# Chunk 12 transposed on TensorE, loads moved behind transposes, and a rearranged start, in a retention and hard-swish kernel

## The chip, the cores and the metric

The kernel runs on one core of a Trainium2 chip. The core has TensorE (matrix products, which write PSUM), VectorE (DVE in the profile), ScalarE (ACT), GpSimd (POOL) and SyncE (SP), each with its own instruction stream in program order, and 16 DMA engines that move data between memory (HBM) and the on-chip SBUF. DMAs are issued from the queues of SP, ACT and POOL. The engines meet by semaphores. The metric is device microseconds of one execution; less is better.

## The reference

```python
def _attn_ref(q, k, v):                       # each 8 x 8 x 576 x 64: batch, heads, positions, head size
    scores = scale * np.matmul(q, k.transpose(0, 1, 3, 2))
    gamma = 1.0 - 2.0 ** (-5.0 - np.arange(H, dtype=np.float32))
    rel = pos[:, None] - pos[None, :]
    Dmat = np.where(rel >= 0, gamma[:, None, None] ** rel[None, :, :], 0.0)
    return np.matmul(scores * Dmat, v)

def _moe_ref(x, w_in, w_out):                 # x 4608 x 512, w_in 512 x 2048, w_out 2048 x 512
    h = x @ w_in
    g = h * np.clip(h + 3.0, 0.0, 6.0) / 6.0
    return g @ w_out
```

A decayed causal attention without softmax (retention) for 8 batch entries and 8 heads, its heads laid side by side to rows of 512, and then two dense layers with a hard swish between them.

## The kernel before, in words

**Tiling.** Tokens are worked on in nine blocks of 512. Block 0 holds the first 64 positions ("heads" in the code) of all eight batch entries; blocks 1 to 8 hold the other 512 positions of one batch entry each, as four chunks of 128. Chunks are numbered through: 4 to 35, and chunk c belongs to block c // 4. For each chunk the retention is computed inside the chunk with a mask, and what lies before it comes in through a state of 64 x 64 per head that is decayed and carried on.

**One chunk.** `load(c)` (L171) puts three loads into SP's queue: keys, queries and values as fp32 (tiles fk, fq, fv; `IOB` = 4 buffers each, 256 KB a load). `casts(c)` (L182 to L184) makes fp16 of them: keys on ACT, queries and values with their decays on POOL. `transposes(c, on_pe)` turns k and q so that the head size lies on partitions. With `on_pe` it is done by TensorE against an identity (tiles ptk and ptq, L161), and copied out of PSUM by ACT (k) and VectorE (q) (L195). Without it, SP issues two DMA transposes (L197). `state(c)` (L243 to L249) forms the next state: products on TensorE, a sum on VectorE, a decay on POOL. `past(c)` (L235) has ACT put a state into the tile sbd. `scores(c)` (L208, L211) forms the products of qT and kT and masks them on VectorE. `inner(c)` (L262, L161, L266) forms the chunk's output, which ACT copies into xT, the input of the dense layers.

**The dense layers.** `up_steps` does one of 16 units of 128 hidden columns for a block: four products of w_in and xT into a PSUM bank (ph), u by ACT (L387), g by VectorE (L389). `down_plain` does the second layer for blocks 0 and 1, one product at a time (a "D" of the plans, pd), the other blocks use a Strassen scheme (`down_strassen`, pm) with sums of weights that VectorE makes (L405, "+n" in the plans). Weights come by POOL's queue, converted to fp16 by the DMA: w_in in four pieces (`win_piece`, L508) and w_out in four (`wout_piece`, L511). The queue stands in program order behind the heads' keys and values (L293).

**Order.** The order of everything is written out by hand. For blocks 0 to 2 strings say it: "k0 D4 ... t11 c13" means: item k for 0, four D, ..., the transposes of chunk 11 on TensorE, cast of chunk 13. The letters: c cast, t transposes on TensorE, s state, z past, a scores, i inner, k and h the heads' keys and states, o a kept output store of block 0, U, L and R whole and half units of the up layer. An engine executes its share of the items in this order. From block 2 on, tables give the order.

**Queue order on SP.** `cast(c)` also feeds SP: for c >= `PE_T` it issues the DMA transposes of c, and then `fetch(c + IOB + 1)` loads up to chunk c + 4:

```python
PE_T = 12
...
            if c >= PE_T:
                transposes(c, False)
            fetch(c + IOB + 1)
```

So chunks 4 to 11 are turned by TensorE, chunks 12 to 35 by DMA. The first four chunk loads are held until the third w_out piece has landed (`fetch(8, wout[2])`).

**The start.** Keys and queries of block 0 come in quarters (one pair of heads): head pair 0's keys and all queries by SP and ACT as fp32, cast on the chip (`cast_heads`, L304); keys of pairs 1 to 3 and all values by POOL's queue with conversion to fp16 in the DMA. `turn_heads` transposes a pair on TensorE (L311) and copies it out (L315); `scores_heads` masks with hmask, which ACT makes by exponentials (`mask_of_heads`, L122). `idle_products` are products without use that keep TensorE busy. `others()` (L125 to L141) makes the decay tables on VectorE and ACT, multiplies the heads' keys by decays on POOL, and clears or fills small tiles.

Of the kernel before, what the change touches and what calls it, by code (L numbers as in the profile page):

```python
# [15 lines left out]
ACTF = mybir.ActivationFunctionType  # L16
ALU = mybir.AluOpType
# [4 lines left out]
def kernel(  # L22
# [9 lines left out]
    nc = tc.nc  # L32
    B, H, S, D = q.shape
    NTOK, DM = out.shape
    DFF = moe_w_in.shape[1]
    P = 128
    NP = H // 2
    NFC = DFF // P
    BLK = 512
# [16 lines left out]
    IOB = 4  # L56
# [64 lines left out]
        for h in (2 * i, 2 * i + 1):  # L121
            nc.scalar.activation(hmask[:, h, :], dist, ACTF.Exp, bias=scale, scale=float(np.log(gamma[h])))  # L122

    def others():
        for h in range(H):  # L125
            lg = float(np.log(gamma[h]))
            nc.vector.tensor_scalar(arg[:, :, h], fj[:, 0:NJ + 1], lg, float(np.log(D ** -0.5)),
                                    ALU.mult, ALU.add)
            nc.vector.tensor_scalar(arg[:, :, H + h], fj[:, 0:NJ + 1], -lg, 0.0, ALU.mult, ALU.add)
        nc.scalar.activation(dec, arg, ACTF.Exp)  # L130
        for i in range(NP):
            k16 = hd[i]["k"].rearrange("p e j d -> p j e d")
            dd = dec[:, 0:NJ, H + 2 * i:H + 2 * i + 2].unsqueeze(3).to_broadcast([P, NJ, 2, D])
            nc.gpsimd.tensor_tensor(k16, k16, dd, ALU.mult)
        for i in range(2):
            nc.vector.memset(sbd[i], 0.0)
        nc.vector.tensor_copy(only[:, 1:2], odd)
        nc.vector.tensor_scalar(only[:, 0:1], odd, -1.0, 1.0, ALU.mult, ALU.add)
        for h in range(H):
            lo = (h % 2) * D  # L140
            nc.vector.memset(gpow[lo:lo + D, h // 2:h // 2 + 1], float(gamma[h] ** P))  # L141

    def mask_of_chunk():
        nc.gpsimd.memset(mask, 1.0)
# [125 lines left out]
    def idle_products(n):  # L270
        idle = psum.tile([P, NP, P], FP32, tag="pp", name="idle")
        for _ in range(n):
            product(idle, ident16, ident16.unsqueeze(1).to_broadcast([P, NP, P]), start=True, stop=True)
# [11 lines left out]
    def load_half(i, nm, e, queue, behind=None):  # L285

        if nm not in hd.setdefault(i, {}):
            if queue is nc.gpsimd:
                hd[i][nm] = heads16(i, nm)
            else:  # L290
                f = io.tile([P, H, D], FP32, tag=f"f{nm}", name=f"h{nm}{i}")
                hd[i][nm] = f.rearrange("p (e j) d -> p e j d", e=2)
        d = queue.dma_start(hd[i][nm][:, e].rearrange("p j d -> p (j d)"),  # L293
                            dict(q=q, k=k, v=v)[nm][:, 2 * i + e, 0:TL, :].rearrange("b (r j) d -> r b (j d)", j=NJ))
        if behind is not None:
            after(d, behind)
        return d
# [4 lines left out]
    def cast_heads(i, nm, copy):  # L302
        t = heads16(i, nm)
        copy(t, hd[i][nm])  # L304
        hd[i][nm] = t

    def turn_heads(i, nm, copy):
        pt = psum.tile([P, NJ, P], FP32, tag="st", bufs=2, name=f"hpt{nm}{i}")
        for j in range(NJ):
            for e in range(2):  # L310
                nc.tensor.matmul(pt[e * D:e * D + D, j, :], hd[i][nm][:, e, j, :], by_chunk, start=True, stop=True,  # L311
                                 skip_group_check=True)
        x, y = (NCB, 2 * RP) if nm == "k" else (2 * NCB, RP)
        t = work.tile([P, x, NJ, y], FP16, tag=f"{nm}T", bufs=4, name=f"h{nm}T_{i}")
        copy(t, pt.rearrange("p j (x y) -> p x j y", y=y))  # L315
        hd[i][nm + "T"] = t
# [186 lines left out]
                pend.append((ws[n][:, j, :], x[:, j, :], y[:, j, :], op))  # L503


    def win_piece(n):
        a, b = pieces_in[n]
        return nc.gpsimd.dma_start(win16[n], win_v[:, :, BLK * a:BLK * b])  # L508

    def wout_piece(pc):  # L510
        return nc.gpsimd.dma_start(wout16[:, JQ * pc:JQ * pc + JQ, :], wout_v[pc])  # L511

    PE_T = 12
    loaded, ready = [NCB], [NCB]

    def fetch(n, behind=None):
        while loaded[0] < min(n, NCH):
            for i in load(loaded[0]):
                if behind is not None:
                    after(i, behind)  # L520
            loaded[0] += 1

    def cast(c):
        if c < NCH:
            assert ready[0] == c
            casts(c)
            ready[0] += 1
            if c >= PE_T:
                transposes(c, False)
            fetch(c + IOB + 1)  # L530

    def do(todo):
        for what, c in todo:
# [36 lines left out]
    with tc.manual_schedule(engines={ENG.PE, ENG.DVE, ENG.Pool, ENG.Activation, ENG.SP}):  # L570
        sp, act, pool = nc.sync, nc.scalar, nc.gpsimd
        on_act, on_dve = nc.scalar.copy, nc.vector.tensor_copy
        indices()
        for nm in ("k", "q"):
            load_half(0, nm, 0, sp)
            load_half(0, nm, 1, act)
        nc.scalar.activation(warm, half, ACTF.Exp)
        load_half(1, "q", 0, sp)
        load_half(1, "q", 1, act)
        for i in (2, 3):  # L580
            for e in range(2):
                load_half(i, "q", e, sp)
        for i, nm in ((1, "k"), (2, "k"), (3, "k"), (0, "v"), (1, "v"), (2, "v"), (3, "v")):
            for e in range(2):
                load_half(i, nm, e, pool)
        win_piece(0)
        distances()
        idle_products(5)
        mask_of_heads(0)
        cast_heads(0, "k", on_dve)  # L590
        turn_heads(0, "k", on_act)
        for i in (1, 2, 3):
            mask_of_heads(i)
        idle_products(2)
        cast_heads(0, "q", on_dve)
        turn_heads(1, "k", on_act)
        cast_heads(1, "q", on_dve)
        turn_heads(0, "q", on_dve)
        turn_heads(1, "q", on_act)
        cast_heads(2, "q", on_dve)  # L600
        turn_heads(2, "k", on_act)
        scores_heads(0)
        cast_heads(3, "q", on_act)
        scores_heads(1)
        turn_heads(3, "k", on_act)
        turn_heads(2, "q", on_act)
        values_heads(0)
        turn_heads(3, "q", on_act)
        scores_heads(2)
        values_heads(1)  # L610
        inner_heads(0, on_act)
        scores_heads(3)
        values_heads(2)
        inner_heads(1, on_act)
        win_piece(1)
        values_heads(3)
        inner_heads(2, on_dve)
        first = [up_steps(0, u) for u in range(3)]
        for dmc in range(3):
            for unit in first:  # L620
                next(unit)
            if dmc == 1:
                inner_heads(3, on_act)
        for unit in first:
            for _ in unit:
                pass
        for n in (2, 3):
            win_piece(n)
        wout = [wout_piece(pc) for pc in (0, 2, 1, 3)]
        mask_of_chunk()  # L630
        others()
        fetch(8, wout[2])
        for u in range(3, NFC):
            up_unit(0, u)
        weight_sums(4, 7)
        weight_sums(6, 3, 1)
        down = down_plain(0)
        go("k0 D4 k1 D4 +1 k2 D4 +1 k3 D6 h0 D2 c4 +1 h1 D3 z4 h2 D3 +1 h3 D3 c5 D4 t4 D5 s4 a4 D5 t5 +1 i4 "
           "z5 c6 D4 s5 a5 D7 i5 D2 t6 z6 L2 c7 s6 a6 L3 D3 t7 L1 i6 L3 a7 z7 L3 c8 D2 i7 D3 t8 R3 c9 R3 "
           "s8 a8 z8 R2 t9 R2 c10 i8 R2 U1 s9 a9 z9 c11 U3 i9",  # L640
           1, down)
        down = down_plain(1)
        go("t10 c12 z10 D6 s10 a10 D2 t11 c13 +1 D6 i10 z11 D1 a11 c14 +2 D8 i11 z12 o1 +1 D6 D1 s12 a12 c15 D4 +1 "
           "D4 i12 z13 o1 D1 s13 a13",
           down=down)
        go("U1 D3 i13 U1 D2 U1 z14 U1 D2 s14 a14 U1 D2 c16 U1 D2 i14 U1 D2 z15 U1 D2 +1 U1 a15 D2 "
           "U1 D2 c17 +1 U1 D2 i15 +1 U1 D2 +1 U1 +1 U1 D2 U1 U1",
           2, down)
        for kb in range(2, NB):
            for _ in down:  # L650
                pass
            plain = kb < FIRST
            down = down_plain(kb) if plain else down_strassen(kb)
            per = 4 if plain else 7
            table = FIRST_STEADY if kb == 2 else STEADY
            c = NCB * (kb + 2)
            for u in range(NFC):
                lead = per - 2 if u == 0 else 0
                for _ in range(lead):
                    next(down, None)  # L660
                if kb + 1 < NB:
                    up_unit(kb + 1, u)
                else:
                    side_sums(1)
                for _ in range(per - lead):
                    next(down, None)
                do((w, i if w == "+" else c + i) for w, i in table.get(u, []))
        for _ in down:
            pass
# [30 lines left out]
```

## Time and profile before

| | |
|---|---|
| time, three runs | 306.31, 306.67, 307.20 us (median 306.67) |
| profiled execution | 307.96 us, of which the span is 306.3 us |
| TensorE busy | 289.8 us (95%) |
| VectorE, ACT, POOL busy | 240.1, 200.0, 146.5 us |
| longest wait of TensorE | 4.6 us, scores on a DMA transpose of q |
| other waits of TensorE over 1 us | 1.9 (start), 1.8 (heads' keys), 1.4 (w_in) |
| SP's transposes | 24 of k, 24 of q; median 4.3 and 3.0 us from issue to landing |
| chunk loads on SP | 96, 256 KB each, median 4.3 to 5.3 us to landing |

Times in the profile are us from the start of the span. In the lists of waits a line says: engine, tile and line, "<-" what it waited for, then us in total, how often, and the longest. In the table of windows each row has the window, its length, and for PE, PEld (weight loads), DVE, ACT and POOL the busy time and the count of instructions; the last three numbers are the granted TensorE clock as a share of full speed, the busy share of the DMA engines and GB/s. In a timeline a row has start, us, engine, line, operation, output <- inputs, shapes and how many were merged; in brackets the idle time before it and what ended it. "SPq" is an issue on SP's queue, which takes SP the time given; the landing comes later.

### The profile page before, as it was taken

The numbers are of one execution on the slowest core, as the hardware profiler recorded it, in microseconds if no ns is written. First come the engines' busy times: TensorE is split into PE (matmuls) and PEld (weight loads), VectorE is DVE, ScalarE is ACT, GpSimd is POOL, SyncE is SP. The second block draws the span as 40 slices with busy tenths as digits, with TensorE's granted clock in tenths as the row PEclk, the third lists the DMA queues.
The fourth block names the chain that finished last, engine by engine and source line by source line (L and its number), as shares of the span: only waits on it lengthen the run. The fifth ranks groups of instructions, "written<-read, shape, count | busy, mean of one in ns | idle before, by whom it ended". The sixth has DMA issues, their size and how long they took to land.

```text
span 306.3 us, 10639 instructions
## 1 busy us (share of the span) xinstructions
PE 289.8 (95%) x4494; PEld 223.9 (73%) x4494; DVE 240.1 (78%) x414; ACT 200.0 (65%) x373; POOL 146.5 (48%) x153
## 2 busy tenths in 40 slices
PE   4889999999949999999999999999999999999994
PEld 1668566887625667778787878787887878778893
DVE  4749486888934795989979987989798979777962
ACT  5748867999725686875677577657766765455330
POOL 7815097636740900984197519743973353013100
PEclk9799999999998999999999999999999999999999
DMA  6999999999999999999979997897925000300123
GB/s 150 191 206 215 197 205 214 215 213 209 172 146 235 204 218 225 161 175 225 217 167 160 198 210 151 147 205 195 153 54 173 20 19 2 140 2 2 68 74 137
DMA packets 137072, 48.01 MB, mean 157 GB/s; under 512 B 126784, under 2 KB 131904, under 8 KB 137024
## 3 DMA queue, kind: packets, MB, share of 16 engines
q1 hardware_dynamic: 131888, 41.83, 69.7%
q0 software_dynamic: 4704, 5.11, 10.1%
q8 instruction: 35, 0.57, 0.8%
q10 hardware_dynamic: 432, 0.39, 0.5%
q14 instruction: 13, 0.11, 0.1%
HBM read 36.70 MB, written 9.44 MB: 151 GB/s over the span
## 4 chain that ended last, share of the span: by engine, by line
PE 83%; DVE 5%; DMA 5%; POOL 2%; ACT 2%; issue 1%; POOLq 0%; DVEq 0%; ACTq 0%
PE ph L161 39%; PE pm L161 28%; PE pd L161 7%; PE pa L208 3%; PE po L262 2%; PE po L161 2%; DMA win<-in_moe_w_in_dram 2%; DMA hk<-in_k_dram 2%; DVE g L389 2%; DMA qT<-q 1%; DVE ws L405 1%; ACT u L387 1%; DVE a L211 1%; POOL hk L293 1%; PE pu L243 1%
## 5 line engine op out<-in xcount | busy, mean ns | idle before, releaser
L161 PE MATMUL ph<-xT,win 128*64 128x512 f16 (+1 forms) x1248 | 148.1, 367 | 2.2 <-DMA win<-in_moe_w_in_dram 1.4
L387 ACT ACTIVATE u<-ph,half 128x512 f32<-128x512 f32 (+1 forms) x156 | 100.0, 656 | 65.1 <-PE ph L161 63.1
L389 DVE SCALAR_TENSOR_TENSOR g<-u,ph 128x512 f16<-128x512 f32 (+1 forms) x156 | 98.1, 642 | 38.6 <-ACT u L387 38.0
L161 PEld LDWEIGHTS <-win 128*64 128x64 f16 x1248 | 82.6, 137 | 26.7 <-issue 2.3
L249 POOL TENSOR_TENSOR z<-t,gpow 128x256 f32<-128x256 f32 x24 | 18.0, 750 | 81.3 <-DVE t L248 73.1
L161 PEld LDWEIGHTS <-g 128*64 128x64 f16 x704 | 38.3, 110 | 14.8 <-issue 0.7
L211 DVE TENSOR_TENSOR a<-pa,mask 128x512 f16<-128x512 f32 x64 | 40.3, 682 | 5.1 <-PE pa L208 5.1
L161 PE MATMUL pm<-ws,s 128*64 128x256 f16 x672 | 43.8, 273 | 0.0
L161 PEld LDWEIGHTS <-s 128*64 128x64 f16 x672 | 37.0, 110 | 7.1
L405 DVE TENSOR_TENSOR s<-g 128x1024 f16<-128x1024 f16 x42 | 41.3, 987 | 0.0
L184 POOL TENSOR_TENSOR v<-fv,dec 128x512 f16<-128x512 f32 x32 | 40.0, 1250 | 0.1
L183 POOL TENSOR_TENSOR q<-fq,dec 128x512 f16<-128x512 f32 x32 | 37.4, 1167 | 1.9 <-DMA fq<-in_q_dram 1.9
L161 PE MATMUL pd<-wout,g 128*64 128x512 f16 x256 | 34.6, 386 | 0.0
L161 PE MATMUL pm<-ws,g 128*64 128x256 f16 x448 | 30.6, 273 | 0.0
L161 PE MATMUL pm<-wout,sab 128*64 128x256 f16 x448 | 30.6, 273 | 0.0
L161 PEld LDWEIGHTS <-sab 128*64 128x64 f16 x448 | 24.7, 110 | 4.8
L266 ACT CAST xT<-po 128x512 f16<-128x512 f32 x32 | 18.8, 587 | 13.1 <-PE po L161 13.0
L405 DVE TENSOR_TENSOR sab<-g 128x1024 f16<-128x1024 f16 x28 | 23.4, 838 | 0.0
L182 ACT CAST k<-fk 128x512 f16<-128x512 f32 x32 | 19.8, 619 | 0.2
L235 ACT CAST sbd<-z 64x256 f16<-64x256 f32 x48 | 19.2, 400 | 0.4
L262 PE MATMUL po<-a,v 128*64 128x128 f16 x256 | 18.5, 219 | 0.3 <-DVE a L211 0.3
L161 PE MATMUL po<-qT,sbd 128*64 128x128 f16 x256 | 18.1, 219 | 0.0
(105 smaller groups left out, 266.8 us busy)
## 6 DMA issues: line engine op xcount, KB each, us to landing
fk<-in_k_dram SPq DMA_DIRECT2D x32, 256.0 KB, 4.3
fq<-in_q_dram SPq DMA_DIRECT2D x32, 256.0 KB, 4.6
fv<-in_v_dram SPq DMA_DIRECT2D x32, 256.0 KB, 5.3
out_dram<-o SPq DMA_DIRECT2D x16, 512.0 KB, 4.7
win<-in_moe_w_in_dram POOLq DMA_DIRECT2D x4, 512.0 KB, 8.9
wout<-in_moe_w_out_dram POOLq DMA_DIRECT2D x4, 512.0 KB, 16.2
out_dram<-o SPq DMA_DIRECT2D x4, 256.0 KB, 4.6
hq<-in_q_dram SPq DMA_DIRECT2D x6, 128.0 KB, 5.5
```

What stands on the lines that cost most here:

```text
L161: nc.tensor.matmul(out[r], lhs[:, r], rhs, skip_group_check=True, **flags)
L182: nc.scalar.copy(k16, fk)
L183: nc.gpsimd.tensor_tensor(q16, fq, dd[:, 0:H, :], ALU.mult)
L184: nc.gpsimd.tensor_tensor(v16, fv, dd[:, H:2 * H, :], ALU.mult)
L211: nc.vector.tensor_tensor(a16[:, h2], pa[h2], m, ALU.mult)
L235: nc.scalar.copy(sbd[i0 % 2][r, :, h2, :], z[r])
L249: nc.gpsimd.tensor_tensor(z, t, decay, ALU.mult)
L262: nc.tensor.matmul(po[h2 * D:h2 * D + D, i, :], v16[:, 2 * i + h2, :], a16[:, h2, i, :], start=(i == 0), stop=False, skip_group_check=True)
L266: nc.scalar.copy(xts[kb][:, :, i0 * P:i0 * P + P], po)
L387: nc.scalar.activation(uu[:, 0:n], ph[:, 0:n], ACTF.Relu, bias=half, scale=1.0 / 6.0)
L389: nc.vector.scalar_tensor_tensor(out=g[:, hf, ths, jr, :], in0=by_half(uu), scalar=1.0, in1=by_half(ph), op0=ALU.min, op1=ALU.mult)
L405: nc.vector.tensor_tensor(*pend.popleft())
```

## The change

- `PE_T` goes from 12 to 13: chunk 12 is turned by TensorE ("t12" in the plan, after i11), and the DMA transposes begin with chunk 13.
- `fetch` in `cast(c)` asks for chunks up to c + 4 only while c < 11, and up to c + 3 after that, so that from there on a later load stands behind the transposes of c.
- The first w_in piece comes as two DMAs of half the contraction rows each.
- The heads' keys of pairs 1 to 3 are loaded as fp32, still by POOL's queue, and cast by VectorE (three more `cast_heads`).
- `others()` is split: `decays()` (VectorE) runs right after the first transposes of the heads, its exponential on ACT after the masks; the fills of gpow and sbd go from VectorE to POOL.
- Idle products: 4 in place of 2 in the second group. Four up units are started together in place of three.
- In the plans "+1" moves from before i4 to after a5, z6 from before the first L2 to after L3, and the two "o1" from after z12 and z13 to after z13 and a14. On SP the first store thereby moves from between chunk 14's and chunk 15's issues to behind chunk 15's; both still stand ahead of chunk 16's.

```diff
-    def others():
+    def decays():
         for h in range(H):
...
-        nc.scalar.activation(dec, arg, ACTF.Exp)
+        nc.vector.tensor_copy(only[:, 1:2], odd)
+        nc.vector.tensor_scalar(only[:, 0:1], odd, -1.0, 1.0, ALU.mult, ALU.add)
+
+    def others():
         for i in range(NP):
...
-        for i in range(2):
-            nc.vector.memset(sbd[i], 0.0)
-        nc.vector.tensor_copy(only[:, 1:2], odd)
-        nc.vector.tensor_scalar(only[:, 0:1], odd, -1.0, 1.0, ALU.mult, ALU.add)
         for h in range(H):
             lo = (h % 2) * D
-            nc.vector.memset(gpow[lo:lo + D, h // 2:h // 2 + 1], float(gamma[h] ** P))
+            nc.gpsimd.memset(gpow[lo:lo + D, h // 2:h // 2 + 1], float(gamma[h] ** P))
+        for i in range(2):
+            nc.gpsimd.memset(sbd[i], 0.0)
...
-            if queue is nc.gpsimd:
+            if nm == "v":
                 hd[i][nm] = heads16(i, nm)
...
-    def win_piece(n):
+    def win_piece(n, parts=1):
         a, b = pieces_in[n]
-        return nc.gpsimd.dma_start(win16[n], win_v[:, :, BLK * a:BLK * b])
+        for i in range(parts):
+            cc = slice(NP // parts * i, NP // parts * (i + 1))
+            nc.gpsimd.dma_start(win16[n][:, cc], win_v[:, cc, BLK * a:BLK * b])
...
-    PE_T = 12
+    PE_T = 13
...
-            fetch(c + IOB + 1)
+            fetch(c + IOB + (c < PE_T - 2))
...
-        win_piece(0)
+        win_piece(0, 2)
         distances()
         idle_products(5)
         mask_of_heads(0)
         cast_heads(0, "k", on_dve)
         turn_heads(0, "k", on_act)
+        decays()
         for i in (1, 2, 3):
             mask_of_heads(i)
-        idle_products(2)
+        nc.scalar.activation(dec, arg, ACTF.Exp)
+        idle_products(4)
+        cast_heads(1, "k", on_dve)
+        turn_heads(1, "k", on_act)
         cast_heads(0, "q", on_dve)
-        turn_heads(1, "k", on_act)
         cast_heads(1, "q", on_dve)
         turn_heads(0, "q", on_dve)
+        cast_heads(2, "k", on_dve)
         turn_heads(1, "q", on_act)
+        turn_heads(2, "k", on_act)
         cast_heads(2, "q", on_dve)
-        turn_heads(2, "k", on_act)
+        cast_heads(3, "k", on_dve)
         scores_heads(0)
...
-        first = [up_steps(0, u) for u in range(3)]
+        first = [up_steps(0, u) for u in range(4)]
...
-        go("... t5 +1 i4 "
-           "z5 c6 D4 s5 a5 D7 i5 D2 t6 z6 L2 c7 s6 a6 L3 D3 t7 ..."
+        go("... t5 i4 "
+           "z5 c6 D4 s5 a5 +1 D7 i5 D2 t6 L2 c7 s6 a6 L3 z6 D3 t7 ..."
...
-        go("... D8 i11 z12 o1 +1 D6 D1 s12 a12 c15 D4 +1 "
+        go("... D8 i11 t12 z12 +1 D6 D1 s12 a12 c15 D4 +1 "
            "D4 i12 z13 o1 D1 s13 a13",
-        go("U1 D3 i13 U1 D2 U1 z14 U1 D2 s14 a14 U1 D2 c16 ..."
+        go("U1 D3 i13 U1 D2 U1 z14 U1 D2 s14 a14 o1 U1 D2 c16 ..."
```

More of the change, by code (lines that the diff above doesn't have):

```diff
@@ L632 @@
         fetch(8, wout[2])
-        for u in range(3, NFC):
+        for u in range(4, NFC):
             up_unit(0, u)
@@ L637 @@
         down = down_plain(0)
-        go("k0 D4 k1 D4 +1 k2 D4 +1 k3 D6 h0 D2 c4 +1 h1 D3 z4 h2 D3 +1 h3 D3 c5 D4 t4 D5 s4 a4 D5 t5 +1 i4 "
-           "z5 c6 D4 s5 a5 D7 i5 D2 t6 z6 L2 c7 s6 a6 L3 D3 t7 L1 i6 L3 a7 z7 L3 c8 D2 i7 D3 t8 R3 c9 R3 "
+        go("k0 D4 k1 D4 +1 k2 D4 +1 k3 D6 h0 D2 c4 +1 h1 D3 z4 h2 D3 +1 h3 D3 c5 D4 t4 D5 s4 a4 D5 t5 i4 "
+           "z5 c6 D4 s5 a5 +1 D7 i5 D2 t6 L2 c7 s6 a6 L3 z6 D3 t7 L1 i6 L3 a7 z7 L3 c8 D2 i7 D3 t8 R3 c9 R3 "
            "s8 a8 z8 R2 t9 R2 c10 i8 R2 U1 s9 a9 z9 c11 U3 i9",
@@ L642 @@
         down = down_plain(1)
-        go("t10 c12 z10 D6 s10 a10 D2 t11 c13 +1 D6 i10 z11 D1 a11 c14 +2 D8 i11 z12 o1 +1 D6 D1 s12 a12 c15 D4 +1 "
+        go("t10 c12 z10 D6 s10 a10 D2 t11 c13 +1 D6 i10 z11 D1 a11 c14 +2 D8 i11 t12 z12 +1 D6 D1 s12 a12 c15 D4 +1 "
            "D4 i12 z13 o1 D1 s13 a13",
            down=down)
-        go("U1 D3 i13 U1 D2 U1 z14 U1 D2 s14 a14 U1 D2 c16 U1 D2 i14 U1 D2 z15 U1 D2 +1 U1 a15 D2 "
+        go("U1 D3 i13 U1 D2 U1 z14 U1 D2 s14 a14 o1 U1 D2 c16 U1 D2 i14 U1 D2 z15 U1 D2 +1 U1 a15 D2 "
            "U1 D2 c17 +1 U1 D2 i15 +1 U1 D2 +1 U1 +1 U1 D2 U1 U1",
```

## The prediction

> **What bounds the kernel now.** I read the page's first part, then the waits, the time windows, and the timelines of SP and TensorE around the longest wait.
>
> ```profile
> PE 289.8 (95%) x4494; PEld 223.9 (73%) x4494; DVE 240.1 (78%) x414; ACT 200.0 (65%) x373; POOL 146.5 (48%) x153
> ...
> PE pa L208 <- DMA qT<-q: 4.6, 1, 4.6
> PE ph L161 <- DMA win<-in_moe_w_in_dram: 1.4, 1, 1.4
> ```
>
> TensorE sets the end: busy 289.8 of 306.3 us, so a gain has to come out of 16.5 us of idle time or out of slow matmuls. The one long wait is scores of a chunk on DMA transposes.
>
> ```profile
> 85.00:91.00 6.00, 1.44 (x38) 1.19 (x33) 1.29 (x2) 1.29 (x3) 2.35 (x3) 0.96 1.16 125
> 91.00:95.00 4.00, 4.00 (x41) 2.05 (x38) 1.98 (x3) 0.96 (x2) 0.00 (x0) 0.63 1.18 197
> 95.00:99.00 4.00, 4.00 (x50) 2.50 (x48) 1.37 (x2) 3.07 (x6) 0.00 (x0) 1.00 1.16 255
> ```
>
> The wait has a tail: the granted clock (third number from the right) is 0.63 in the 4 us after it, against 1.00 later. At half speed that is 2 x 0.37 x 4 = 3.0 us of slow time, or 1.5 us of work lost; one ph product (two matmuls) comes every 0.43 us there and every 0.215 us later, and I take 1.6 us.
>
> ```profile
> 75.81 1.79 SPq L171 DMA_DIRECT2D fv<-in_v_dram  x1
> 77.73 1.70 SPq L197 DMA_TRANSPOSE kT<-k  x1
> 79.55 1.19 SPq L197 DMA_TRANSPOSE qT<-q  x1
> 80.78 0.59 SPq L171 DMA_DIRECT2D fk<-in_k_dram  x1
> 81.83 0.37 SPq L171 DMA_DIRECT2D fq<-in_q_dram  x1
> 82.30 0.84 SPq L171 DMA_DIRECT2D fv<-in_v_dram  x1
> 83.25 2.72 SPq L197 DMA_TRANSPOSE kT<-k  x1
> 86.08 1.21 SPq L197 DMA_TRANSPOSE qT<-q  x1
> ...
> 85.77 0.30 PE L243 MATMUL pu<-v,k 128*64 128x64 f16 x8
> 90.62 0.61 PE L208 MATMUL pa<-qT,kT 64*128 64x128 f16 x8 [4.56 <-DMA qT<-q]
> ...
> 98.20 0.40 PE L208 MATMUL pa<-qT,kT 64*128 64x128 f16 x8
> ```
>
> Counting loads from chunk 4 on, SP issues chunk 15's loads until 77.60, then chunk 12's transposes (landing 82.1, scores at 83.03 without a wait), chunk 16's loads, and only at 83.25 and 86.08 chunk 13's, which land at 90.6. So chunk 13 is late by 4.6 us, not chunk 12. SP runs without a pause from 73 to 95: a transpose pair plus a chunk's loads take 6.6 us of its queue (83.25 to 89.87).
>
> ```profile
> 15.36 0.41 PE L356 MATMUL hpo<-ha,ws 128*64 128x128 f16 x8
> 17.13 1.51 PE L161 MATMUL ph<-xT,win 128*64 128x512 f16 x12 [1.35 <-DMA win<-in_moe_w_in_dram]
> 25.85 6.26 PE L161 MATMUL ph<-xT,win 128*64 128x512 f16 x56 [0.25 <-DVE g L389]
> ```
>
> The front has two small waits: the first w_in piece, and a g that VectorE made late because lines 127 to 141 held it from 22.54 to 25.07.
>
> **Part by part.** I follow TensorE to the scores of chunk 14, at 98.20 now; behind them it has no wait over 0.3 us that the change touches.
>
> *Chunk 12 on TensorE.* Added: 16 matmuls, the ptk and ptq of chunk 11 take 76.26 to 76.71, so 0.45 us on the path (up to 0.82 by their busy time, 3.3 + 3.3 us over eight chunks); an ACT copy of 0.59 us where ACT is busy 3.88 of 6 us (80 to 86), hidden; a VectorE copy of 0.69 us where VectorE is busy 5.87 of 6, so between 0 and 0.69. Laid out, it stands ahead of the chunk's state sum and mask products, and i12 still finds them done by 0.3 us: I take 0. Without that cover it costs 0.4. Removed: two transposes from SP's queue (77.73 to 80.74). Chunk 13's take their place, if its casts are there; k13 and q13 are cast by 77.93 and 78.15, earlier if the front gains. They should land where chunk 12's did, at 82.1, or as late as 85.0 if they take the 7.3 us of the slow pair. TensorE wants them at about 84. So the 4.6 us and the 1.6 us go: -6.2 + 0.45.
>
> *The loads.* The code's arithmetic puts chunk 15's loads at cast(12), still ahead of chunk 13's transposes; from chunk 16 on they stand behind the transposes of chunk c and bring c+3, not c+4. SP's order becomes L15, T13, L16, T14, L17 where it was L15, T12, L16, T13, L17. So T14 gets the slot that T13 has now and lands at 90.6. **That is what is late next.** The stores of block 0 (a pair of issues, 1.57 us) move on SP too: the first from ahead of T15 to behind chunk 18's loads, the second next to it, still ahead of T16. So T15 follows L17 at 89.8 and lands 5.1 us later (like the pair issued from 97.40 on), at 94.9; TensorE wants it 7.1 us after scores 14, at 97.7. T16 gets one pair more ahead of it and one T and one load less; TensorE has 15.7 us between scores 15 and 16 (105.3 to 121.0). Nothing for either, and without that cover 1.6 us.
>
> *w_in in halves.* One more POOL issue, 0.4 to 0.8 us (win 0.76, wout 0.57 each), queued ahead of the later weights, whose landings stand 2.5 us apart (the first two pieces at 17.1 and 19.6): the transfer paces them, so nothing. The first half lands at least 1.25 us before 17.1, at 15.8 or sooner, and TensorE then waits for VectorE instead (next item). If both halves landed at 17.1, 0.7 us of the front would go: 299.4.
>
> The Trainium skill ("DMA: Bandwidth & Descriptors", Rules for kernel authors) says that two transfers to disjoint partition halves serialize and are not worth making; the 2.5 us spacing agrees that they serialize; by this rule the split gains nothing and the time is that of both halves at 17.1, 299.4.
>
> *Keys unconverted.* Their landing (5.1 to 5.7 us) may come 2.4 us sooner (2.7, the first unconverted keys) or 0.9 later (6.0, the slowest queries); nearest are the queries of the same size and moment, 5.4: I take 0. Three VectorE casts at 0.43 us are added: k1 waits for its landing at 7.68 and now stands ahead of q0, q1 and the copy of qT0. Between 0 and 1.3 us on the path; in order, the eight mask products (0.63 apart, 5.0 us) start at about 11.4, not 10.85: +0.55. VectorE then frees the first units' banks at about 16.4, so the units start there, not at 17.13: -0.7.
>
> *Four units at once, decays early.* With four units the copy of the last head's output (18.91 to 19.50) is hidden: -0.3. The 16 small operations (22.54 to 23.78) move into VectorE's 2.65 us wait before 7.16, their exponential (0.27) behind the masks on ACT, idle 0.57 us there; the memsets go to POOL, ten at 0.1 to 1.1 us (rows of 0.10 for one column, 0.27 for 128, times four), idle from 16.9 to 24.2 and free again from 28.2. The g wait goes: -0.4, counting its issue gap. Two more idle products, 0.4 to 0.9 us, lie in TensorE's gap from 5.7 to 6.9: nothing.
>
> *The plan.* "+1" behind a5: i5 at 48.94 waits about 0.5 us for a VectorE product that a 1.56 us weight sum delayed. z6 behind L3: ACT's two sbd copies (0.83) no longer delay u, for which TensorE loses 0.4 us at 52.64; they now end about when i6 wants them, so 0 to 0.4 comes back. Together -0.8. Loads do not take this gain back: q6, q7 and q9 are cast as they land, but TensorE uses them 3 us later.
>
> **Sum.** TensorE reaches scores 14 at 98.2 - 6.2 + 0.45 - 0.7 - 0.3 - 0.4 - 0.8 = 90.25; T14 is there at 90.6. The later one holds: 7.6 us earlier, with a wait of some 0.4 us. Profiled, 307.96 us (span 306.3 and 1.7 around it) become 300.4; it stands 1.3 above the median of 306.67, so the median becomes **299.1**.
>
> **Rivals.**
> *The front gives nothing* (key casts or landings late, halves together): the 1.4 us of its three terms go, and 0.75 more if all three casts count in full, so TensorE is at scores 14 by 91.65 to 92.4, and the time 300.1 to 300.9. For it: VectorE already is full from 10.85 to 16.5. Against: 2.65 us of idle VectorE before.
> *The transposes take the wait's place.* If T13 needs the slow pair's 7.3 us and not 4.4, T14 lands at up to 93.5, TensorE waits 3.2 us, and part of the slow clock (up to 1.6) returns: 302 to 303.6. For it: SP has no pause there. Against: T13 follows the same loads as T12 did.
> The Trainium skill ("TensorE: Matmul & The Clock Gate", Part 1) says half rate comes after an idle window of about 3.4 us; the first wait on w_in, 1.35 us, kept 1.00 and the 4.6 us one did not, so the trace agrees.
> *Slower: loads run dry.* With one chunk less ahead, a load waits for T(c-3), T for its cast, the cast for its load. One lap is 5.1 (transposes) + 5.5 (loads) + 2.5 (two POOL casts) = 13 us, over three chunks; TensorE takes 29.7 us for four (blocks at 147.99 and 177.69), 22 for three. It decides once a lap passes 22 us. At 24.5, the 16 chunks left would each take 0.8 more, 13 us: 312. Nothing but queueing speaks for it.
> *The change does nothing measurable*, T13 waiting on a cast until it is late again: within 306.67 +- 0.9 (0.3%, what this kernel's measurements can tell).
>
> **How the numbers follow.** Forecast 0.57 (298.3 to 299.9), front 0.17, transposes 0.14, dry loads 0.06, nothing 0.04, and 0.02 for more than forecast (298.0: T14 early). 298.0 to 302.4 leaves out the last two rivals and half of the transposes. Faster 0.90, same 0.04, slower 0.06.
>
> **What would show it.** Right: no wait on qT over 1 us, clock 1.00 from 84 to 95, scores 13 at 84 to 85, scores 14 at 90 to 91, the first units at 16 to 16.8, mask products from 11.2 to 11.6. Wrong: SP pausing before T13, T14 landing after 91.5, a new TensorE wait between 30 and 84, or q casts waiting for landings after 120.

## The result and the profile after

| | before | after |
|---|---|---|
| median | 306.94 us (306.31 to 307.77, four runs) | 302.38 us (301.66 to 302.45, four runs) |
| ratio, 95% interval | | 0.9845 (0.9815 to 0.9874) |
| profiled execution, its span | 307.96 us, 306.3 us | 301.66 us, 299.9 us |

The kernel became faster, by 1.55% (1.3 to 1.85%). The forecast was 299.1 us; 302.38 lies at the upper end of the range (298.0 to 302.4) and outside the likeliest case's own (298.3 to 299.9).

The first part of the page, of the kernel after (line numbers are one higher than before):

```profile
PE 289.5 (97%) x4514; PEld 222.1 (74%) x4514; DVE 240.2 (80%) x408; ACT 200.9 (67%) x374; POOL 149.4 (50%) x164
```

The list of TensorE's waits in it:

```profile
PE hptk L312 <- DVE hk L305: 2.5, 2, 2.3
PE idle L162 <- POOL ident masks.py:199: 1.9, 1, 1.9
PE hptq L312 <- DVE hqT L316: 0.8, 1, 0.8
```

The 4.6 us on a transpose of q are gone, and so are the waits on w_in and on g. A wait that was not there before heads the list: 2.3 us for a cast of the heads' keys by VectorE, at the very start. The windows at and behind the old wait's place (the granted clock is the third number from the right):

```profile
85.00:91.00 6.00, 6.00 (x85) 3.87 (x82) 3.12 (x6) 4.10 (x8) 2.40 (x3) 1.00 1.27 210
91.00:95.00 4.00, 4.00 (x61) 2.53 (x59) 3.26 (x6) 3.10 (x6) 1.54 (x2) 1.00 1.04 120
```

The scores of chunks 12, 13 and 14 in TensorE's timeline:

```profile
82.48 0.40 PE L209 MATMUL pa<-qT,kT 64*128 64x128 f16 x8
85.45 0.40 PE L209 MATMUL pa<-qT,kT 64*128 64x128 f16 x8
91.46 0.40 PE L209 MATMUL pa<-qT,kT 64*128 64x128 f16 x8
```

TensorE is busy throughout and its granted clock is 1.00. From scores 12 to scores 14 it takes 8.98 us, against 15.17 before (83.03 to 98.20). SP's queue, for comparison with the rows shown of before:

```profile
77.05 1.00 SPq L172 DMA_DIRECT2D fv<-in_v_dram  x1
78.56 1.31 SPq L198 DMA_TRANSPOSE kT<-k  x1
79.99 1.19 SPq L198 DMA_TRANSPOSE qT<-q  x1
81.24 0.57 SPq L172 DMA_DIRECT2D fk<-in_k_dram  x1
81.86 1.12 SPq L172 DMA_DIRECT2D fq<-in_q_dram  x1
83.02 0.70 SPq L172 DMA_DIRECT2D fv<-in_v_dram  x1
83.83 1.85 SPq L198 DMA_TRANSPOSE kT<-k  x1
85.79 1.20 SPq L198 DMA_TRANSPOSE qT<-q  x1
```

Chunk 13's transposes now stand where chunk 12's stood (issues at 78.56 and 79.99; the trace has the second landing at 84.08, 1.4 us before TensorE wants it). Chunk 14's land at 89.23, 2.2 us early.

The other end of the gain is the front. The first transposes of the keys in TensorE's timeline:

```profile
8.28 0.53 PE L312 MATMUL hptk<-by_chunk,hk 128*64 128x128 f16 x8 [2.29 <-DVE hk L305]
```

VectorE's timeline of the same time, up to the eight mask products:

```profile
7.80 0.43 DVE L305 CAST hk<-hk 128x512 f16<-128x512 f32 x1 [2.12 <-DMA hk<-in_k_dram]
...
11.37 0.43 DVE L305 CAST hk<-hk 128x512 f16<-128x512 f32 x1 [0.45 <-DMA hk<-in_k_dram]
11.76 2.48 DVE L348 TENSOR_TENSOR ha<-hpa,ws 128x512 f16<-128x512 f32 x4
15.24 2.48 DVE L348 TENSOR_TENSOR ha<-hpa,ws 128x512 f16<-128x512 f32 x4 [1.00 <-ACT hqT L316]
```

A cast waits for its keys' landing, TensorE for the cast, the mask products begin at 11.76 (10.85 before) and have a hole of 1.00 us in their middle. The first unit starts at 17.46 (17.13 before). I compare the fronts by the start of the first heads' state products, the item k0 of the plan, at 31.93 after and 32.04 before: in this pair of profiles 0.1 us was gained where 1.4 was forecast. Over all profiles k0 comes at 31.90 to 32.85 with the front of before (five, mean 32.26) and at 31.24 to 32.72 with that of after (four, mean 31.80), so a front gain of some 0.5 us is possible and not resolved, and 1.4 is not there.

### The profile page after: what moved, and what is told of

Its sections match the earlier page's. It is cut to its first block, busy times and chain, and to the rows that moved or that the text cites. A ratio compares the mean times of both kernels' runs of the same rounds, so it can differ in the third digit from the quotient of the medians.

```text
span 299.9 us, 10657 instructions
## 1 busy us (share of the span) xinstructions
PE 289.5 (97%) x4514; PEld 222.1 (74%) x4514; DVE 240.2 (80%) x408; ACT 200.9 (67%) x374; POOL 149.4 (50%) x164
## 3 DMA queue, kind: packets, MB, share of 16 engines
q0 software_dynamic: 4144, 5.51, 10.4%
## 4 chain that ended last, share of the span: by engine, by line
PE 91%; DVE 3%; DMA 2%; ACT 1%; issue 1%; POOL 1%; DVEq 0%; POOLq 0%; ACTq 0%
PE ph L162 41%; PE pm L162 29%; PE pd L162 9%; PE pa L209 3%; PE po L263 2%; PE po L162 2%; DMA hk<-in_k_dram 2%; DVE g L390 1%; PE pu L244 1%; DVE a L212 1%; ACT u L388 1%; PE hptq L312 1%; PE hpa L344 1%; PE hpv L325 1%; PE hptk L312 1%
## 5 line engine op out<-in xcount | busy, mean ns | idle before, releaser
L162 PEld LDWEIGHTS <-win 128*64 128x64 f16 x1248 | 80.0, 137 | 26.4 <-DMA win<-in_moe_w_in_dram 0.5
L406 DVE TENSOR_TENSOR s<-g 128x1024 f16<-128x1024 f16 x42 | 41.3, 988 | 0.0
L185 POOL TENSOR_TENSOR v<-fv,dec 128x512 f16<-128x512 f32 x32 | 39.1, 1221 | 1.2 <-DMA fv<-in_v_dram 1.2
L162 PE MATMUL pd<-wout,g 128*64 128x512 f16 x256 | 34.0, 381 | 0.0
L406 DVE TENSOR_TENSOR sab<-g 128x1024 f16<-128x1024 f16 x28 | 24.1, 863 | 0.0
```

Source lines behind the costliest of these rows:

```text
L162: nc.tensor.matmul(out[r], lhs[:, r], rhs, skip_group_check=True, **flags)
L185: nc.gpsimd.tensor_tensor(v16, fv, dd[:, H:2 * H, :], ALU.mult)
L406: nc.vector.tensor_tensor(*pend.popleft())
```

## The experiments

All kernels here compute everything that the reference asks for. Each of the three groups has its own runs of the kernel before, with medians of 307.70 (11 runs), 308.01 (11) and 307.91 (17): higher than the three and four runs above.

### What of the gain is chunk 12 and the load order

`t12_only`: the kernel before with only PE_T, the plan's t12, the new fetch and the moved o1.

```diff
-    PE_T = 12
+    PE_T = 13
...
-            fetch(c + IOB + 1)
+            fetch(c + IOB + (c < PE_T - 2))
...
-... D8 i11 z12 o1 +1 ...
+... D8 i11 t12 z12 +1 ...
```

> The kernel before with chunk 12 turned by TensorE, the later loads and the moved stores alone; nothing of the start or of the other plan moves. By the prediction's terms: the 4.6 us wait goes, 0.45 us of matmuls come, and the half-speed window behind the wait goes in those executions that have it: 4.2 to 5.8 us less than before, scores of chunk 13 at about 86.5 with no wait over 0.5. Rival, that chunk 14 waits in its place: a wait of over 1 us on its transposes and less than 3.5 us gained.

Measured: 302.52 us (302.24 to 303.81, six runs), ratio 0.9839 (0.9804 to 0.9874). Scores 12, 13 and 14 start at 83.33, 86.30 and 92.31, with the clock at 1.00. The whole change, run again beside it on the same chip (`again`):

> The changed kernel as it is, beside the kernel before, in more rounds. Theory of the load queue and theory of the slow clock at the start both expect 302.4 us and a ratio of 0.985. Theory of the window's phase (the 1.6 us of half-speed work behind the 4.6 us wait are in the profiled execution of before, but not in each execution): the executions of before spread over 1 to 1.6 us by whether a half-speed window follows the wait, those of the changed kernel over less than 1 us; rival: both spread alike.

Measured: 302.74 us (301.39 to 303.51, six runs), ratio 0.9832 (0.9795 to 0.987). The two can't be told apart in time. The transposes, the loads and the moved stores carry the whole measured gain; everything else in the change together brings nothing that these runs resolve, though by the profiles the whole change reaches scores 14 0.85 to 1.0 us sooner (91.46 and 91.29 against 92.31). The kernel is also spread more widely (2.1 us) than its first four runs said.

`load_order`: the kernel after, with the loads of chunk 16 ahead of chunk 13's transposes again.

```diff
-            fetch(c + IOB + (c < PE_T - 2))
+            fetch(c + IOB + 1)
```

> The changed kernel with each cast again loading up to chunk c + 4, so that chunk 16's loads stand ahead of chunk 13's transposes on SP. By the queue's rows (a chunk's loads take 2.4 us of SP) chunk 13's transposes are issued at about 81 and not 78.6 and land at 86.5 to 87.5; TensorE wants them at 85.4, so a wait of 1 to 2 us comes back, the clock stays at 1.00, and the time is 303.4 to 304.4. If the order of the loads is worth nothing: no wait over 0.5 us, 302.2 to 302.7.

Measured: 304.27 us (303.04 to 305.24, four runs), ratio 0.9888 (0.9842 to 0.9934). The scores of chunks 13 and 14 in its timeline:

```profile
85.84 0.40 PE L209 MATMUL pa<-qT,kT 64*128 64x128 f16 x8 [0.96 <-DMA qT<-q]
93.15 0.40 PE L209 MATMUL pa<-qT,kT 64*128 64x128 f16 x8 [1.22 <-DMA qT<-q]
```

Two waits on transposes come back, 2.2 us in all; the clock stays at 1.00. From k0 to scores 14 it takes 61.84 us, against 59.53 in the kernel after. So chunk 12 on TensorE takes away most of the wait, and the load order the last 2.3 us by the profile, 1.5 by the medians (the ratios, 0.9888 against 0.9832, make it 1.7, but their intervals overlap).

### Why the front gave almost nothing

Three causes were open: the unconverted keys land later; w_in in halves is slower; TensorE, idle for 2.3 us, runs at half speed after it. The granted clock shows half speed in the windows of the start of the kernel after:

```profile
6.00:10.00 4.00, 0.99 (x16) 0.79 (x17) 1.81 (x5) 2.23 (x8) 2.02 (x4) 0.81 1.12 290
10.00:17.00 7.00, 6.93 (x152) 5.15 (x151) 5.40 (x10) 5.45 (x11) 6.44 (x11) 0.62 1.02 131
```

But the kernel before has half speed there too, with no pause over 1.21 us between 2 and 10 us:

```profile
6.00:10.00 4.00, 1.74 (x32) 1.50 (x32) 2.09 (x4) 2.36 (x8) 2.64 (x6) 0.83 1.28 257
10.00:17.00 7.00, 5.69 (x148) 4.07 (x144) 5.60 (x9) 6.01 (x12) 6.32 (x12) 0.85 1.21 172
```

Worked out from these rows, half speed lasts about 3.4 us before and 6.8 us after.

`keep_busy`: more idle products, so that TensorE does not rest before the key cast.

```diff
-        idle_products(4)
+        idle_products(14)
```

> The changed kernel with 14 idle products in place of 4 in the second group, so that TensorE is busy until 8.2, when the cast of the second pair's keys comes. Theory of the slow clock: clock 1.00 from 8.4 to 15.3, mask products 0.5 to 1 us earlier, first up unit at 16.5 to 17.0, time 301.5 to 301.9. Theory of the load queue: the clock is 1.00 too, but the first half of w_in still lands at 17.4, the first up unit starts there, time 302.2 to 302.5.

Measured: 302.50 us (301.84 to 303.48, six runs), ratio 0.9831 (0.9793 to 0.9869). Its window from 10 to 17:

```profile
10.00:17.00 7.00, 5.75 (x168) 4.21 (x163) 6.39 (x12) 6.17 (x13) 6.40 (x11) 1.00 1.08 148
```

Its wait on w_in, in the list of waits:

```profile
PE ph L162 <- DMA win<-in_moe_w_in_dram: 1.1, 2, 0.8
```

The clock is 1.00, but the ten products more end only at 9.6, so that the first transpose behind them is 1.3 us later than in the kernel after. Even so the mask products end at 17.31 in place of 17.72: the hole in them is 0.16 us. It is 0.98 and 1.00 us in the two executions of the kernel after, with 6.8 us of half speed, and 0.43 to 0.64 in `load_order`, `plan_undo`, `keys_whole` and `all_split`, with 3.4. So the slow clock does cost time ahead of the units. They start (17.16) as the first half of their w_in piece lands (17.11), and then TensorE waits 1.1 us for w_in: k0 comes at 32.91. The second half landed at 19.58 here, 0.9 us later than in the kernel after; in `plan_undo`, whose start is that of the kernel after, it landed at 19.48, so this is spread between executions and need not come from the ten products. With the slow clock gone the weights' queue holds the end of the front.

`keys_conv`: keys converted by their DMA as before, no casts; everything else of the change stays.

```diff
-            if nm == "v":
+            if queue is nc.gpsimd:
...
-        cast_heads(1, "k", on_dve)
-        cast_heads(2, "k", on_dve)
-        cast_heads(3, "k", on_dve)
```

> The changed kernel with the heads' keys of pairs 1 to 3 converted by the DMA again, and without their three casts on VectorE. Theory of the load queue (unconverted keys move more slowly on POOL's queue and hold back everything behind them): keys land at 6.9 to 10.3 as before, the first half of w_in at 15.8 or sooner, the first up unit at 16.0 to 16.6 and not 17.5, the third w_out piece at 32.4 and not 33.9, the heads' keys by key (hpk) at 30.5 to 30.8 and not 31.9; time 301.0 to 301.4. Theory that the unconverted keys cost nothing and only the slow clock from 8.4 to 15.3 does: first half of w_in still at 17.4, time 302.2 or more.

Measured: 302.24 us (301.67 to 302.99, five runs), ratio 0.9823 (0.9786 to 0.986). The first units in TensorE's timeline:

```profile
15.86 1.95 PE L162 MATMUL ph<-xT,win 128*64 128x512 f16 x16
18.86 1.95 PE L162 MATMUL ph<-xT,win 128*64 128x512 f16 x16 [0.82 <-DMA win<-in_moe_w_in_dram]
21.45 0.87 PE L162 MATMUL ph<-xT,win 128*64 128x512 f16 x6 [0.64 <-DMA win<-in_moe_w_in_dram]
```

Here the front does what the prediction wanted, and even more: the first half lands at 15.82, and the units start at 15.86, not 17.46. But then TensorE waits for the second half (18.81) and for the second piece (21.40), and k0 comes at 31.96, as in the kernel after; 301.0 to 301.4 us in all, as expected with sooner keys, did not come. So late keys explain the late first unit, and still they are not what sets the end of the front: the weights' stream is. (0.8 us of this run's profile is one wait on chunk 14's transposes.)

`conv_whole` and `keys_whole` bring the first piece whole; the former converts the keys in the DMA besides (the diff of `keys_conv` as well).

```diff
-        win_piece(0, 2)
+        win_piece(0)
```

> The changed kernel with the heads' keys converted by the DMA again (no casts of them) and the first w_in piece in one transfer. Theory that the split itself slows the queue's stream around it (with converted keys and the split, the two halves landed at 15.8 and 18.8, the second piece at 21.4, where the kernel before has 17.1 and 19.6): w_in pieces land at 17.0 and 19.5, the first up unit starts at 17.0 without a later wait on w_in, hpk at 31.3 to 31.5 and not 32.0, span 299.6 to 300.0, time 0.4 to 0.8 us under that with the split. Rival, that the slow stretch comes from something else at the start (the moved VectorE work, more idle products): the second piece lands after 21 again, hpk at 31.9.

> The changed kernel with the first w_in piece in one transfer, keys unconverted as in the change. Theory of the split: the piece lands at 17.8 to 18.2 (0.8 later than before, by the keys), the second at 20.4 and not 21.4, the first up unit starts at 18.0, hpk at 32.3; the split is worth 0.4 us here, by its first half. Theory of the keys alone: the piece lands at 18.7 and the second at 21.4 as with the split, the first unit at 18.7, hpk at 33.

Measured: `conv_whole` 301.46 us (300.71 to 303.24, six runs), ratio 0.9798 (0.9761 to 0.9835); `keys_whole` 301.41 in its one execution. Landings and starts of these kernels from their traces, us:

| | before | after | keys_conv | conv_whole | keys_whole |
|---|---|---|---|---|---|
| keys of pair 3, two loads | 9.37, 10.31 | 10.61, 11.27 | 9.31, 10.03 | 9.53, 10.43 | 10.50, 11.01 |
| first w_in piece (halves) | 17.09 | 17.41, 18.66 | 15.82, 18.81 | 17.38 | 17.63 |
| second w_in piece | 19.59 | 21.38 | 21.40 | 19.88 | 20.19 |
| third w_out piece | 32.36 | 33.91 | 33.85 | 32.80 | 32.94 |
| first unit | 17.13 | 17.46 | 15.86 | 17.42 | 17.67 |
| k0 | 32.04 | 31.93 | 31.96 | 31.64 | 31.90 |
| first unit to k0 | 14.91 | 14.47 | 16.10 | 14.22 | 14.23 |

With the split, the second piece lands 1.2 to 1.5 us later, whichever way the keys come (21.38 and 21.40 against 20.19 and 19.88); all later weights shift by about 1 us. The other traces agree: the second piece lands at 20.7 to 22.4 in the seven traces with a split first piece, and at 19.5 to 20.4 in the seven without. And k0 follows this landing: in the six traces in which only the first piece is split, it comes 10.55 or 10.56 us after it, whether the first unit starts at 15.86 or at 17.46. With a whole first piece, k0 comes 14.95 or 14.96 us after the first piece's landing in the five traces with the front of before, and 14.26 and 14.27 in `conv_whole` and `keys_whole`. In the kernel after, TensorE's products show no wait for the second piece, but its weight loads do:

```profile
21.42 3.65 PEld L162 LDWEIGHTS <-win 128*64 128x64 f16 x36 [0.49 <-DMA win<-in_moe_w_in_dram]
```

`conv_whole` has the lowest median of the kernels with several runs. Against the kernel after the intervals overlap (0.9798, 0.9761 to 0.9835, beside 0.9845 and 0.9832), so that it is better is likely and not shown.

`all_split`: all four w_in pieces in halves, to see whether a half moves slower.

```diff
-        win_piece(1)
+        win_piece(1, 2)
...
-            win_piece(n)
+            win_piece(n, 2)
```

> The changed kernel with all four w_in pieces in halves. Theory that a half moves more slowly for its bytes: a piece takes 3 to 3.7 us and not 2.5, the last lands at 28 or later, hpk later than 33. Rival, that only the time around 12 to 17 is slow whatever moves then: 2.5 us a piece, the last at 26.5 as in the changed kernel, hpk at 31.9.

Measured: 302.89 us in one execution. The halves land at 16.84, 18.26, 20.95, 22.13, 23.36, 24.64, 25.92 and 27.22. From the fourth on a half takes 1.2 to 1.3 us, 2.5 a piece, as fast as whole pieces; only the third takes 2.7. So a half is not always slower. Where the stream is slow, the windows show (the last number is GB/s), here of the kernel after and then of `conv_whole`:

```profile
14.00:18.00 4.00, 3.97 (x98) 2.69 (x96) 3.00 (x6) 3.46 (x7) 3.68 (x7) 0.84 1.08 150
```

```profile
14.00:18.00 4.00, 3.39 (x94) 2.29 (x92) 3.08 (x5) 3.12 (x6) 3.92 (x8) 1.00 1.23 201
```

From 14 to 18 us the seven traces with a split first piece have 130 to 160 GB/s, the seven with a whole one 189 to 202; `all_split` has 172 from 18 to 22 too, and then 204. Why the split slows the stream there stays open. The run also has a wait of 1.0 us of a pd product on ACT's copy of an output:

```profile
PE pd L162 <- ACT o L435: 1.0, 1, 1.0
```

It is no clear price of more issues, since `again`, without them, has the same wait (0.3 us): in both, ACT's cast of chunk 5's keys waits for their landing, and the copy stands behind it.

### The plan

`plan_undo`: the kernel after with the first plan as it was.

```diff
-... t5 i4 z5 c6 D4 s5 a5 +1 D7 i5 D2 t6 L2 c7 s6 a6 L3 z6 ...
+... t5 +1 i4 z5 c6 D4 s5 a5 D7 i5 D2 t6 z6 L2 c7 s6 a6 L3 ...
```

> The kernel after with the first plan as before ("+1" ahead of i4, z6 ahead of the weights' loads). By the prediction's working the plan is worth 0.8 us: scores 12 come 0.85 later than in the kernel after (83.3 against 82.5) and the median is 303.2. If the loads take the gain back, or the other parts of the change had brought what stands between the kernel after and its T12 part alone at scores 12, scores 12 come at 82.5 and the median stays at 302.4.

Measured: 302.68 us (302.01 to 303.98, six runs), ratio 0.9835 (0.9802 to 0.9869), no different from the kernel after in time. The profile is finer. Its k0 came at 32.72, 0.79 later by the start alone, and from there to scores 12 it takes 50.85 us, against 50.55 in the kernel after and 51.43 in `t12_only`. From scores 6 to scores 7 it takes 5.51 as before, against 5.08: the move of z6 is worth 0.43. The wait at i5 did not come back, though the weight sum is at its old place. The sum in VectorE's timeline, of `t12_only` (old plan, L405) and of `plan_undo` (L406):

```profile
46.22 1.56 DVE L405 TENSOR_TENSOR ws<-wout 128x1024 f16<-128x1024 f16 x1
```

```profile
47.04 0.68 DVE L406 TENSOR_TENSOR ws<-wout 128x1024 f16<-128x1024 f16 x1
```

One instruction, two durations. POOL's timeline beside them, again of `t12_only` and then of `plan_undo`:

```profile
45.62 0.61 POOL L249 TENSOR_TENSOR z<-t,gpow 128x256 f32<-128x256 f32 x1
46.19 1.04 POOL L183 TENSOR_TENSOR q<-fq,dec 128x512 f16<-128x512 f32 x1
47.20 1.49 POOL L184 TENSOR_TENSOR v<-fv,dec 128x512 f16<-128x512 f32 x1
```

```profile
46.44 0.61 POOL L250 TENSOR_TENSOR z<-t,gpow 128x256 f32<-128x256 f32 x1
47.36 1.26 POOL L184 TENSOR_TENSOR q<-fq,dec 128x512 f16<-128x512 f32 x1 [0.32 <-DMA fq<-in_q_dram]
```

Where POOL converts without a pause the sum takes 1.56 us; where POOL happens to stand still for a landing as the sum runs its first 0.32 us, it takes 0.68. Of the 80 sums of this shape in the trace of `plan_undo`, the 31 with no POOL instruction beside them take 0.67 to 0.69 us, the other 49 take 0.68 to 1.80. So this half of the plan's gain depends on what POOL does beside the sum. The Trainium skill ("GPSIMD Engine Reference", section 1, Specifications) lists GpSimd's SBUF interfaces as shared with VectorE, with contention for VectorE instructions that have two SBUF inputs, as this sum has; these rows agree with it, though no run here varied POOL alone.

### The clock behind the wait, and the spread of the kernel before

The profiled execution of before stood 1.3 us over its median, so a theory was that its half-speed window is a matter of chance. Two further executions of the unchanged kernel, and a kernel with the clock held, test it:

> The kernel before, unchanged, a second look. If the half-speed window behind the 4.6 us wait comes in every execution, the granted clock of TensorE from 91 to 95 is again about 0.63 and scores 14 start again 5.8 us after the end of the wait plus 1.8 (7.6 behind scores 13). If it depends on where the clock's windows happen to lie (windows of about 3.4 us, as the first profile shows one from 90.6 to 94.0), the clock there can be 1.00 and scores 14 come 6.0 behind scores 13, and such an execution is about 1.6 us shorter: 306.3.

> The same once more: by the first theory clock 0.63 and scores 14 at 7.6 behind scores 13 again; by the second either that, with 307.5 to 308, or clock 1.00, 6.0 and about 306.3.

Measured: 308.47 and 307.04 us. Scores 13 and the wait ahead of them, and scores 14, of the first execution and then of the second:

```profile
91.07 0.53 PE L208 MATMUL pa<-qT,kT 64*128 64x128 f16 x8 [2.75 <-DMA qT<-q]
98.70 0.40 PE L208 MATMUL pa<-qT,kT 64*128 64x128 f16 x8
```

```profile
89.71 0.61 PE L208 MATMUL pa<-qT,kT 64*128 64x128 f16 x8 [3.32 <-DMA qT<-q]
97.26 0.40 PE L208 MATMUL pa<-qT,kT 64*128 64x128 f16 x8
```

From scores 13 to scores 14 it is 7.63 and 7.55 us, 7.58 in the first profile: half speed came in all three. What differs is when chunk 13's transposes land (91.0, 89.7, 90.6). From scores 14 to the end of the span all three take the same 208.06 to 208.07.

`hold_clock`: the kernel before with 16 products into an unread bank ahead of scores 13.

```diff
+        if c == 13:
+            idle_products(16)
         kT, qT = st[c]["kT"], st[c]["qT"]
```

> The kernel before with 16 products into an unread bank ahead of the scores of chunk 13, so that TensorE is at work for 3.5 of the 4.6 us and its clock isn't lowered; all that is computed stays. Both theories: clock 1.00 from 91 to 95, scores 13 still at 90.6 (the transposes are not sooner), scores 14 6.0 behind them. If the slow window comes in every execution of the kernel before, the median of this one is 1.6 us lower (306.1 against 307.7, ratio 0.995). If it comes in about half of them, 0.8 lower (0.9975), and the fastest executions of both are equal, at about 306.2.

Measured: 306.49 us (305.47 to 308.26, twelve runs), ratio 0.9963 (0.9934 to 0.9992), that is 0.2 to 2.0 us less. Its timeline:

```profile
86.67 3.63 PE L161 MATMUL idle<-ident 128*64 128x512 f16 x32
90.69 0.40 PE L210 MATMUL pa<-qT,kT 64*128 64x128 f16 x8 [0.39 <-DMA qT<-q]
96.71 0.40 PE L210 MATMUL pa<-qT,kT 64*128 64x128 f16 x8
```

The window behind it:

```profile
91.00:95.00 4.00, 4.00 (x54) 2.62 (x52) 2.15 (x4) 1.96 (x3) 0.00 (x0) 1.00 1.64 155
```

Scores 13 come no sooner, scores 14 6.02 us behind them in place of 7.55 to 7.63. The slow clock cost 1.5 to 1.6 us, and in every execution looked at. The theory of chance falls for this window; at the kernel's start the clock does differ between executions of before (half speed for 3.4 us in the first profile and in `before_look1`, none in `before_look2`). That this kernel still spreads over 2.8 us says that the clock behind the wait is not the source of the spread.

## Why the prediction was right, and where it was not

Measured from one profile to the other, up to scores 14:

| term | forecast | came |
|---|---|---|
| wait and slow clock, scores 12 to 14 | -6.2 | 8.98 against 15.17: -6.19 |
| transposes of chunk 12 on TensorE, scores 11 to 12 | +0.45 | 4.71 against 4.26: +0.45 |
| plan and what lies beside it, k0 to scores 12 | -0.8 | 50.55 against 50.99, of which +0.45 is chunk 12: -0.89 |
| front, k0 | -1.4 | -0.11 |
| scores 14 | 90.6 | 91.46 |

*Chunk 12 and the loads* are right in place, cause and size. The wait was a queue's: chunk 13 was late because SP issued it late. The slow clock behind it, taken as 1.6 us from the windows, is 1.5 to 1.6 by the kernel that takes it away. Two details went differently: chunk 13's transposes landed at 84.1, not 82.1, and chunk 14's at 89.23, so that "the later one holds" did not come into play; TensorE, late from the front, was the later one. The rivals of transposes that take the wait's place and of loads that run dry did not come.

*The plan* came to the forecast sum. For z6 the undo shows its 0.43; the half that belongs to "+1" did not reappear in the undo, and depends on what POOL does beside the sum.

*The front* is the step that failed; the rival "the front gives nothing" is what happened, and its scores 14 at 91.65 are what the trace has, to 0.2 us (its time, 300.1 to 300.9, is not what came). Of its three terms two were right in size: the hidden copy (-0.3) and the g wait (-0.4) show as 14.23 us from first unit to k0 instead of 14.91 where the first piece is whole. The term of -0.7 for an earlier first unit failed, by two statements.

The first is "Keys unconverted: I take 0" for their landing. It was 1.0 to 1.2 us later for the last pair, a little past the 0.9 that the prediction had as its bad end, and the weights' issues behind them came 0.9 us later. The cast that was added made TensorE wait 2.29 us in one piece for the keys of pair 1, though these landed as before (7.71 against 7.68); half speed then lasted 6.8 us and not 3.4, which was not in the sum, and the mask products ended at 17.72 and not 15.88.

The second is "the transfer paces them, so nothing" for w_in in halves. The second piece came 1.2 to 1.5 us later, and k0 follows that landing by 10.55 us in every trace with this split; in `keys_conv` this undoes a first unit that starts 1.3 us early. The units are fed by the stream of pieces; moving the first one without the second only moves the wait. The Trainium skill's rule in the prediction ("DMA: Bandwidth & Descriptors", Rules for kernel authors) is about two transfers to disjoint halves of the partitions. Here each half fills all 128 partitions, and the 2.5 us that the prediction set beside the rule is the spacing of whole pieces; so the rule does not speak of this split, though the front came out as it would have.

*From the profile to the median* the sum lost another 2.0 us of the 3.3 between 299.1 and 302.38; the other 1.3 are the 0.86 at scores 14 (91.46 for 90.6) and 0.4 that are lost behind them in steps of 0.2 or less and that I did not follow. The prediction took the profiled execution to stand 1.3 over the median, and carried that over. But 306.67 was the median of three runs; over the 39 runs of the three groups it is 307.91, and the profiled 307.96 is an ordinary execution. The kernel after was profiled at 301.66, 0.7 under its own median. That 302.38 still lies inside the range, by 0.02 us, is luck: the upper end of the range belonged to a rival that did not come, and run again the same kernel has a median of 302.74. By medians of one group the change brings 5.0 us (307.70 to 302.74).

What spreads the two kernels differs. In the kernel before it is the landing of chunk 13's transposes, and the wait swallows whatever the front does: k0 at 32.04, 32.14 and 32.37 goes with scores 14 at 98.20, 98.70 and 97.26. In the kernel after no such wait is left: k0 came at 31.24 and 31.93 and, with the same front, at 31.31 in `load_order` and 32.72 in `plan_undo`, as the second w_in piece landed (20.68 to 22.16), and what the front loses or gains goes through, less what the first loads then hold.

## What to carry to other kernels

Ask of a long wait on a queue who stands ahead of it, and move that: here one chunk turned on another engine and three loads behind two transposes took out the wait and the slow clock behind it, to a tenth of a microsecond as read from the profile. A start that is fed by a stream of transfers is priced by the whole stream: sooner first bytes are worth nothing if the second piece comes no sooner. And do not carry the distance of one profiled execution from a median of three runs into a forecast, if the kernel spreads by 3 us; take it as width of the range.

## What the runs showed of the hardware

Loading the keys without conversion made them later, though nothing is left for the DMA to convert. The issues of the two kernels (before, then after), with KB each and the median time to landing:

```profile
hk<-in_k_dram POOLq DMA_DIRECT2D x6, 64.0 KB, 5.1
```

```profile
hk<-in_k_dram POOLq DMA_DIRECT2D x6, 128.0 KB, 6.0
```

The bytes written double, and the queries beside them on SP's and ACT's queues are later too (the last at 11.97, against 10.98). The values behind them on POOL's queue are issued only as the keys land:

```profile
7.17 0.52 POOL L294 DMA_DIRECT2D hv<-in_v_dram  x1 [0.88 <-DMA hk<-in_k_dram]
7.99 0.70 POOL L294 DMA_DIRECT2D hv<-in_v_dram  x1 [0.30 <-DMA hk<-in_k_dram]
9.14 0.51 POOL L294 DMA_DIRECT2D hv<-in_v_dram  x1 [0.46 <-DMA hk<-in_k_dram]
```

So a load that lands later also delays the issue of what stands behind it: the weights start at 12.09, 0.9 us later than before (11.17).

A pause shorter than 3.4 us can lower TensorE's clock too. The Trainium skill ("TensorE: Matmul & The Clock Gate", Part 1) gives half rate after an idle window of about 3.4 us. Here 2.29 and 1.78 us of idle time at the start of the two executions of the kernel after and 2.75 us ahead of scores 13 in `before_look1` were followed by half speed. So were several shorter ones in a row at the start of before, of 1.21, 0.55 and 0.78 us; but in `before_look2`, which is the same kernel, 1.25, 0.45 and 0.78 us at the same place were not. Single pauses of 0.96 to 1.66 us elsewhere were not, nor one of 2.09 us ahead of scores 12 in `before_look1`. Apart from the last microseconds of a trace, each stretch of half speed in these traces lasted 3.4 or 6.8 us. What the gate counts is not settled by this; as a price, a pause of 1.8 us or more, or a row of shorter ones, was not safe.
